# The decay sums' store moved from SyncE's DMA queue to GpSimd's

## The chip, the cores and the metric

One core of a Trainium2 chip runs the whole program once. Its engines are TensorE (PE, with its weight loads as PEld), VectorE (DVE), ScalarE (ACT), GpSimd (POOL) and SyncE (SP). SP, ACT and POOL also issue DMAs, each from its own instruction stream; all DMAs are carried by the same 16 DMA engines. The metric is the device time of one execution in microseconds, as the median of the runs.

## The reference

A causal attention with a decay bias on 8 batches of 8 heads (576 positions, head size 64) feeds a gated feed-forward layer on all 4608 tokens (model size 512, inner size 1536):

```python
s_pos = np.maximum(s, 0.0)
cum = np.cumsum(s_pos, axis=-1)
bias = -(cum[:, :, :, None] - cum[:, :, None, :])
scores = np.where(causal, -1000000000.0, scores + np.minimum(bias, 0.0))
attn = softmax(scores)
x = (attn @ v) as (tokens, 512)
out = (sigmoid(x @ w_gate) * (x @ w_val)) @ w_out
```

The change concerns `cum`: one row of 576 running sums for each of the 64 heads.

## The kernel before

The program is written as one long Python function; a scheduler then decides the order of the instructions on each engine from the data dependencies, the buffers and its own estimate of times, within the marks that the code sets (`high_priority`, `keep_in_program_order`, `issue_after`). A line that moves to another engine can therefore change the order on all engines. The order that results is quoted below where it counts.

*Start.* L108 loads `s` (64 rows of 576) with SP. L162, L164 and L166 on DVE clip it, sum it along the row and subtract the middle value; the result is `rel`. L167 stores `rel` into the DRAM tensor `cum_d`. Head 0 takes its row straight from `rel` (L451, POOL copies row 0 to all 128 partitions). Every later head i loads its row from `cum_d` into partition 0 of a tile `cr` (L447, SP) and L451 spreads it. `rel`, `s_sb`, `cum` and the first `vsq` tiles share the two buffers of the tag `rl`.

*Attention.* `n_load` (L596, SP) brings q and k of a pair of heads, `load_v` (L463, L464, SP) brings v. For batch 0 (8 heads) `n_prep`, `n_s`, `n_max`, `n_turn` and `n_av` work in float32: transposes on PE (L614, evacuated on ACT by L618 to L621), scores (L631), a fused add and minimum on DVE (L643), the exponential on ACT (L644), transposes (L653, L654) and the products with v (L662). Later batches use float16 pairs: scores L489 and L491, DVE L529, ACT L530, products L562 to L567. v's squares (L184 loads on POOL's queue, L186 on ACT) give a scale for each batch.

*Weights.* The weights come as 64-bit floats. `load_weight` loads a block: for the gate and value matrices 128 columns of each, 512 KB and 512 KB, into one staging buffer. Blocks 0 and 1 are loaded by SP (L284), block 0 into `ws`, block 1 into a part of `w2all` that is not yet in use; the later ones by ACT's queue (L286, and L279 for the first half of a w_out block, with the staging buffers `t2f`, `w2all` and `ws` in turn). `decode_weight` (L298 on ACT, L299 to L301 on DVE) makes 32-bit floats of them, `column_bound` (L310 on PE, L313 on DVE) finds a scale, and `split_weight` (L337 on ACT, L338 on DVE) writes a high and a low float16 part. There are 12 blocks of gate and value and 6 of w_out.

*Feed-forward.* `ffn_in` multiplies a group of 256 tokens with one block (L714), a unit of 24 products or more, into a PSUM tile `gv` that has two buffers; L719 on ACT takes the tanh, and L721 on DVE multiplies and so empties the tile. For the first two groups L721 writes into `t2f`. `ffn_out` (L745) multiplies with w_out. Group 0 and 1 start while heads 9 and up are still in attention and weights still come in.

*Order at the start on SP.* The calls at the end of the function (L884 on) issue `n_load(0)`, the two weight blocks and `load_v(0)`; the scheduler put L167 between the two loads of block 1. SP issues in order, and an issue that waits holds back all behind it. [...]

Of the kernel before, what the change touches and what calls it, by code (L numbers as in the profile page):

```python
# [25 lines left out]
def tile_attention_then_gated_ffn(  # L26
# [11 lines left out]
    nc = tc.nc  # L38
# [97 lines left out]
    cum_d = dp.tile([NH, S], F32, name="cum_d")  # L136
# [27 lines left out]
    nc.vector.tensor_tensor_scan(cum, sp_sb, zero, 0.0, ALU.add, ALU.add)  # L164
    rel = wp.tile([NH, S], F32, tag="rl", name="rel")
    nc.vector.tensor_scalar(rel, cum, cum[:, S // 2 : S // 2 + 1], -1.0, ALU.subtract, ALU.mult)  # L166
    nc.sync.dma_start(cum_d, rel)  # L167


    vch = H * S * D // P // S  # L170
# [958 lines left out]
```

## Time and profile before

| | us |
|---|---|
| median of 3 runs | 1143.78 |
| lowest and highest | 1140.69, 1146.3 |
| the profiled execution | 1143.07 |
| its span, first to last instruction | 1141.3 |
| PE busy | 1091.1 |
| DVE busy | 829.2 |
| ACT busy | 753.0 |
| POOL busy | 201.2 |
| mean granted TensorE clock | 0.99 |

The span is that of the profiled execution, and all times of the trace count from its start. A row of the timeline has the start in us, the duration in us, the engine (SPq, ACTq and POOLq are their DMA issues), the line, the operation, what it writes and reads, and in brackets how long the engine idled before it and what ended that wait. A DMA's issue is shorter than the DMA: the data land later. The chain of waits follows the work that ended last back from the last instruction, each step to what released it.

### The profile page before, as it was taken

The numbers are of one execution on the slowest core, as the hardware profiler recorded it, in microseconds if no ns is written. First come the engines' busy times: TensorE is split into PE (matmuls) and PEld (weight loads), VectorE is DVE, ScalarE is ACT, GpSimd is POOL, SyncE is SP. The second block draws the span as 40 slices with busy tenths as digits, with TensorE's granted clock in tenths as the row PEclk, the third lists the DMA queues.
The fourth block names the chain that finished last, engine by engine and source line by source line (L and its number), as shares of the span: only waits on it lengthen the run. The fifth ranks groups of instructions, "written<-read, shape, count | busy, mean of one in ns | idle before, by whom it ended". The sixth has DMA issues, their size and how long they took to land.

```text
span 1141.3 us, 30312 instructions
## 1 busy us (share of the span) xinstructions
PE 1091.1 (96%) x11796; PEld 854.8 (75%) x11796; DVE 829.2 (73%) x2357; ACT 753.0 (66%) x1474; POOL 201.2 (18%) x471
## 2 busy tenths in 40 slices
PE   6897878899999999999999999999999999999998
PEld 4776766757787787788777777778877887787775
DVE  6758989876787777766565577777777779682854
ACT  5868667767786777676656577768776666343533
POOL 3302101022232222221111112212121212000000
PEclk9999889999999999999999999999999999999999
DMA  9776896997989798775736469787977664200000
GB/s 270 215 206 140 180 165 144 183 186 163 174 176 173 158 177 162 155 152 116 169 66 149 103 152 164 150 166 156 179 134 164 145 117 93 41 20 2 20 1 37
DMA packets 445357, 157.62 MB, mean 138 GB/s; under 512 B 403551, under 2 KB 435295, under 8 KB 445214
## 3 DMA queue, kind: packets, MB, share of 16 engines
q1 hardware_dynamic: 418974, 128.17, 57.6%
q10 hardware_dynamic: 23040, 16.78, 5.0%
q0 software_dynamic: 3200, 10.75, 2.6%
q8 instruction: 92, 1.51, 0.5%
q14 instruction: 51, 0.42, 0.1%
HBM read 56.92 MB, written 9.58 MB: 58 GB/s over the span
## 4 chain that ended last, share of the span: by engine, by line
PE 70%; DMA 9%; DVE 8%; issue 5%; ACT 4%; SPq 2%; POOL 1%; ACTq 0%; POOLq 0%; DVEq 0%
PE gv L714 33%; PE o L745 21%; PE tv L831 3%; PE s L491 3%; PE s L489 2%; DMA v<-in_v_dram 2%; PE ta L831 1%; DVE e L529 1%; PE av L564 1%; PE av L562 1%; PE av L563 1%; PE na_ps L662 1%; DMA T<-qk 1%; DMA w2all<-in_moe_w_out_dram 1%; DMA x<-x 1%
## 5 line engine op out<-in xcount | busy, mean ns | idle before, releaser
L714 PE MATMUL gv<-x,w 128*128 128x256 f16 (+3 forms) x6336 | 553.9, 245 | 9.8 <-DVE t2f L721 8.8
L714 PEld LDWEIGHTS <-w 128*128 128x128 f16 x6336 | 480.2, 98 | 63.4 <-issue 12.0
L745 PE MATMUL o<-w2all,h 128*128 128x512 f16 x1296 | 313.9, 379 | 1.9 <-ACT h L729 1.9
L530 ACT ACTIVATE e<-e,em 128x576 f32<-128x576 f32 x280 | 153.1, 556 | 88.8 <-DVE em L529 86.0
L745 PEld LDWEIGHTS <-h 128*128 128x128 f16 x1296 | 123.4, 98 | 109.1 <-ACT h L729 2.3
L511 POOL TENSOR_SCALAR_AFFINE_SELECT rl<-rl 128x128 f32<-128x128 f32 (+1 forms) x240 | 88.4, 369 | 499.2 <-DVE em L529 456.2
L529 DVE CUSTOM_DVE_ANT_0 e<-s,rl,qkcf 128x576 f32<-128x576 f32 x280 | 151.2, 544 | 28.8 <-PE s L491 12.8
L729 ACT ACTIVATE h<-t,hsc 128x256 f16<-128x256 f32 x192 | 96.3, 503 | 92.7 <-DVE t L721 90.4
L719 ACT ACTIVATE th<-gv,scb 128x256 f32<-128x256 f32 (+3 forms) x264 | 99.0, 403 | 65.5 <-PE gv L714 53.9
L539 DVE SCALAR_TENSOR_TENSOR p<-e,p 128x384 f16<-128x384 f32 x224 | 103.2, 499 | 41.1 <-ACT p L534 40.3
L721 DVE SCALAR_TENSOR_TENSOR t<-th,gv 128x256 f32<-128x256 f32 x168 | 69.7, 415 | 63.9 <-ACT th L719 63.8
L534 ACT ACTIVATE p<-e 128x1152 f16<-128x1152 f32 x112 | 111.9, 1000 | 3.4 <-DMA pt<-p 0.9
L730 DVE SCALAR_TENSOR_TENSOR h<-t,hsc,h 128x256 f16<-128x256 f32 x192 | 93.4, 487 | 27.4 <-ACT h L729 25.0
L562 PE MATMUL av<-v,pt 128*128 128x65 f16 x560 | 67.7, 193 | 2.5 <-DMA pt<-p 2.5
L451 POOL PARTITION_BROADCAST cr<-cr x63 | 59.4, 949 | 55.9 <-ACT th L719 21.1
L489 PE MATMUL s<-T 128*128 128x288 f16 (+2 forms) x246 | 64.5, 280 | 3.8 <-DVE em L529 3.0
L563 PE MATMUL av<-v,pt 128*128 128x64 f16 x560 | 67.7, 192 | 0.0
L564 PE MATMUL av<-v,pt 128*128 128x65 f16 x560 | 67.6, 194 | 0.0
L491 PE MATMUL s<-T 128*128 128x288 f16 (+2 forms) x246 | 61.5, 277 | 4.0 <-DMA T<-T 4.0
L562 PEld LDWEIGHTS <-pt 128*128 128x128 f16 x560 | 52.5, 98 | 8.3 <-DMA pt<-p 3.4
L563 PEld LDWEIGHTS <-pt 128*128 128x128 f16 x560 | 52.5, 97 | 4.5
L564 PEld LDWEIGHTS <-pt 128*128 128x128 f16 x560 | 52.7, 97 | 0.2
(209 smaller groups left out, 1539.9 us busy)
## 6 DMA issues: line engine op xcount, KB each, us to landing
v<-v SPq DMA_DIRECT2D x56, 162.5 KB
v<-in_v_dram SPq DMA_DIRECT2D x64, 128.0 KB
out_dram<-io POOLq DMA_DIRECT2D x32, 256.0 KB, 3.4
T<-T SPq DMA_DIRECT2D x82, 72.0 KB
t2f<-in_v_dram SPq DMA_DIRECT2D x20, 288.0 KB
qk<-in_q_dram SPq DMA_DIRECT2D x17, 288.0 KB
qk<-in_k_dram SPq DMA_DIRECT2D x17, 288.0 KB
w2all<-in_moe_w_gate_dram ACTq DMA_DIRECT2D x7, 512.0 KB
```

What stands on the lines that cost most here:

```text
L491: nc.tensor.matmul(ps[:, : b_ - a], lhs, T[i][:, 2, a:b_], start=False, stop=not mask)
L529: nc.vector.tensor_tensor_reduce(e, ps, r, c, MASKED, ALU.add, ALU.min, acc)
L530: nc.scalar.activation(e_t[t][:, :w], e_t[t][:, :w], AF.Exp, bias=acc, scale=-1.0)
L534: nc.scalar.activation(p_s[h_][:, 0], e_s[h_], AF.Copy, scale=PSCALE)
L539: nc.vector.scalar_tensor_tensor(flat[:, LOW[t] * P : (LOW[t] + t) * P], e_t[t][:, : t * P], PSCALE, flat[:, kb * P : (kb + t) * P], ALU.m ...
L562: nc.tensor.matmul(AV[i][:, t], hi, v_[:, D : 2 * D + 1], start=kb == 0, stop=False)
L563: nc.tensor.matmul(AV[i][:, t, 0:D], hi, v_[:, 0:D], start=False, stop=False)
L564: nc.tensor.matmul(AV[i][:, t], lo, v_[:, D : 2 * D + 1], start=False, stop=False)
L714: nc.tensor.matmul(ps[:, gv, a:e], w1[f][:, cc, gv, wl], x_of(b, cc)[:, xl, c0 + a : c0 + e], start=(c == 0), stop=(c == 3 * NC - 1))
L719: nc.scalar.activation(th[:, a:e], ps[:, 0, a:e], AF.Tanh, scale=scb[b][:, f : f + 1])
L729: nc.scalar.activation(h[:, 0], t2, AF.Copy, scale=hsc[:, f : f + 1])
L745: mm = nc.tensor.matmul(ps[:m], h[:, hl, tt * P : tt * P + m], w2[f][:, wl], start=(f == 0 and c == 0), stop=(f == NF - 1 and c == 2))
```

## The change

L167 is issued by GpSimd instead of SyncE. Nothing else in the source changes; what is computed and the bytes moved are the same.

```diff
     rel = wp.tile([NH, S], F32, tag="rl", name="rel")
     nc.vector.tensor_scalar(rel, cum, cum[:, S // 2 : S // 2 + 1], -1.0, ALU.subtract, ALU.mult)
-    nc.sync.dma_start(cum_d, rel)
+    nc.gpsimd.dma_start(cum_d, rel)
```

The scheduler finds a new order for the whole front of the program. On SP, at the start (`nqk` is q or k of a pair of heads, `v_0` and `v_1` are v of the first two pairs, `cr` the rows of sums):

```order
 L284 DMA w2all<-in_moe_w_gate_dram 128x4x256
-L167 DMA cum_d<-rel 64x576
 L284 DMA w2all<-in_moe_w_val_dram 128x4x256
 L463 DMA v_0_159<-in_v_dram 128x4x64 x2
 L464 DMA v_0_159<-in_v_dram 64x2x64
+L463 DMA v_1_256<-in_v_dram 128x4x64
 L596 DMA nqk_251<-in_q_dram 96x6x64 x2
 L596 DMA nqk_251<-in_k_dram 96x6x64 x2
-L463 DMA v_1_256<-in_v_dram 128x4x64 x2
+L463 DMA v_1_256<-in_v_dram 128x4x64
 L464 DMA v_1_256<-in_v_dram 64x2x64
 L447 DMA cr_196<-cum_d 1x576
```

L167 is gone from between the two loads of block 1, and one of the loads of `v_1` stands ahead of the second pair's q and k. L167 now stands on POOL, directly ahead of head 0's L451 and of the first `vsq` load.

On ACT, where the fourth and fifth of w_out's blocks are loaded (into `w2all` and `t2f`), before:

```order
L534 ACTIVATE p_0_81<-e_79 128x768
L719 ACTIVATE th_8_1735<-gv_8_1710,scb_1272 128x256
L279 DMA t2f<-in_moe_w_out_dram 128x8x128
L286 DMA t2f<-in_moe_w_out_dram 128x8x128
L337 ACTIVATE w2all<-io,wscale 128x1024
L502 ACTIVATE rl_2784<-cr_2678,qkcf_2664 128x576
L502 ACTIVATE rl_2915<-cr_2795,qkcf_2664 128x576
L279 DMA w2all<-in_moe_w_out_dram 128x8x128
L286 DMA w2all<-in_moe_w_out_dram 128x8x128
```

and of the change:

```order
L534 ACTIVATE p_0_81<-e_79 128x768
L279 DMA w2all<-in_moe_w_out_dram 128x8x128
L286 DMA w2all<-in_moe_w_out_dram 128x8x128
L583 ACTIVATE x_4_2746<-xq_2260 128x640
L298 ACTIVATE io<-ws_146 128x1024
L279 DMA t2f<-in_moe_w_out_dram 128x8x128
L286 DMA t2f<-in_moe_w_out_dram 128x8x128
L719 ACTIVATE th_8_1735<-gv_8_1710,scb_1272 128x256
```

The `w2all` load has changed places with the `t2f` load.

On DVE, the rows from unit 10 to unit 11 of the first token group (L721 empties a unit's PSUM tile), before:

```order
L721 SCALAR_TENSOR_TENSOR t2f<-th_10_1793,gv_10_1768 128x256
L299 TENSOR_SCALAR w2all<-wa_147 128x1024
L300 SCALAR_TENSOR_TENSOR io<-io,w2all 128x1024
L300 SCALAR_TENSOR_TENSOR wa_147<-wa_147,w2all 128x1024
L721 SCALAR_TENSOR_TENSOR t2f<-th_11_1821,gv_11_1796 128x256
```

and of the change, from the second L300 on:

```order
L300 SCALAR_TENSOR_TENSOR wa_147<-wa_147,w2all 128x1024
L573 TENSOR_SCALAR er_2992<-av_2951 128x5
L529 ISA e_79,em_0_2923<-s_0_2901,rl_2784,qkcf_2664 128x64
L529 ISA em_0_2923 128x1
L338 SCALAR_TENSOR_TENSOR w2all<-io,wscale,w2all 128x1024
L301 SCALAR_TENSOR_TENSOR wa_147<-w2all,wa_147 128x1024
L574 RECIPROCAL er_2992<-er_2992 128x5
L313 TENSOR_SCALAR wj_1897,wtot_1896<-wps_1887 128x128
L539 SCALAR_TENSOR_TENSOR p_1_82<-e_80,p_1_82 128x384
L539 SCALAR_TENSOR_TENSOR p_1_82<-e_80,p_1_82 128x512
L547 SCALAR_TENSOR_TENSOR p_1_82<-e_80,p_1_82 128x2x64
L721 SCALAR_TENSOR_TENSOR t2f<-th_11_1821,gv_11_1796 128x256
```

Ahead of this piece, and behind unit 10's L721, the change also has L299 and the L529 of two other tiles. More rows of attention and of the weights stand between the two L721.

On PE the last difference between the two programs, and its end:

```order
 L714 MATMUL gv_5_5366<-x_143,w_5_71 128x256
-L714 LDWEIGHTS w_5_71
-L714 MATMUL gv_5_5366<-x_143,w_5_71 128x256
-L714 LDWEIGHTS w_5_71
-L714 MATMUL gv_5_5366<-x_2620,w_5_71 128x256
-L714 LDWEIGHTS w_5_71
-L714 MATMUL gv_5_5366<-x_2620,w_5_71 128x256
 L489 LDWEIGHTS T_5052
 L489 MATMUL s_4_5341<-T_5052 128x288
```

Three products of unit 5 of the fourth group (`gv_5_5366`) have moved behind the scores of a head; behind this place PE's order is the same in both.

## The prediction, made before the changed kernel was run

> **What bounds the kernel now.** I first read the head of the page for the span, then a table by stage, to see where TensorE is without work. The table cuts the span where the kind of work changes; its columns are the stretch in us, its length, busy time and instruction count of PE, PEld, DVE, ACT and POOL, the granted clock, the DMA share and GB/s.
>
> ```profile
> span 1141.3 us, 30312 instructions
> ```
>
> ```profile
> core 0: us, PE busy (x) PEld busy (x) DVE busy (x) ACT busy (x) POOL busy (x), PEclk, DMA share, GB/s
> 0.00:100.00 100.00, 81.37 (x580) 65.41 (x580) 68.89 (x191) 73.02 (x150) 26.25 (x60) 0.97 0.77 216
> 100.00:160.00 60.00, 48.64 (x527) 41.42 (x526) 58.40 (x166) 46.25 (x74) 5.08 (x8) 0.94 0.78 158
> 160.00:250.00 90.00, 78.15 (x787) 59.02 (x787) 76.60 (x224) 64.53 (x121) 11.76 (x24) 0.96 0.89 174
> 250.00:350.00 100.00, 97.47 (x1186) 74.48 (x1185) 74.37 (x224) 74.19 (x152) 25.98 (x56) 1.00 0.89 174
> 350.00:960.00 610.00, 608.13 (x7013) 479.90 (x7013) 438.67 (x1311) 418.07 (x821) 125.38 (x314) 1.00 0.72 146
> ```
>
> The reader is to see three things. From 350 to 960 us PE is busy 608.13 of 610: that stage only passes on what comes into it. TensorE's idle time lies before 250 us: 18.63 + 11.36 + 11.85 = 41.84 us of the 250. And from 100 to 160 us the full engine is DVE, 58.40 of 60. So whatever this change does is worth what it does to those 41.84 us. The order of instructions bears this out: the two programs differ on every engine at the front, but the last difference on PE lies in the sixth up-projection unit of the fourth token group, whose bank is emptied by the eighteenth L721 outside the first two groups, below; behind it both issue the same instructions in the same order. A gain or loss made before 350 us arrives at the end almost whole, and none can arise after it except by chance.
>
> ```profile
> 349.98 0.41 DVE L721 SCALAR_TENSOR_TENSOR t<-th,gv 128x256 f32<-128x256 f32 x1
> ```
>
> Now the place of the edit: the first 25 us.
>
> ```profile
> 4.74 0.51 SPq L284 DMA_DIRECT2D w2all<-in_moe_w_gate_dram  x1
> 7.67 0.48 SPq L167 DMA_DIRECT2D cum_d<-rel  x1
> 8.20 0.59 SPq L284 DMA_DIRECT2D w2all<-in_moe_w_val_dram  x1
> ...
> 11.60 3.41 SPq L596 DMA_DIRECT2D nqk<-in_q_dram  x1
> ```
>
> ```profile
> 0.74 3.10 DMA s_sb<-in_s_dram
> ...
> 8.20 7.67 DMA w2all<-in_moe_w_val_dram
> ```
>
> ```profile
> 15.89 1.12 ACT L298 ACTIVATE w2all<-w2all 128x1024 f32<-128x1024 f32 x1 [3.56 <-DMA w2all<-in_moe_w_val_dram]
> ```
>
> SP's queue stands still from 5.25 (4.74 + 0.51) to 7.67, because L167 waits for DVE to finish `rel`; the value half of the second weight block, next in the queue, is issued at 8.20. In the chain that ended last its transfer lasts 7.67 us, and ScalarE idles 3.56 us for it before decoding the block, with head 0's exponentials queued behind. So the wait that the edit removes lies on the path.
>
> **The change part by part.** *The wait on SP.* Without L167 the load is issued at about 5.25, 2.95 us sooner. [...] The best end is that it lands 2.95 us sooner, at 12.9. The other end comes from what SP's DMA queue had to do meanwhile. These are the bytes that it moved in 0 to 8 us and in 8 to 13 us (the columns are packets, MB, share of the engines), and what was issued on it in the first:
>
> ```profile
> q1 hardware_dynamic: 3204, 1.50, 71.8%
> ...
> ws<-in_moe_w_gate_dram SPq DMA_DIRECT2D x1, 512.0 KB
> ws<-in_moe_w_val_dram SPq DMA_DIRECT2D x1, 512.0 KB
> w2all<-in_moe_w_gate_dram SPq DMA_DIRECT2D x1, 512.0 KB
> nqk<-in_q_dram SPq DMA_DIRECT2D x2, 144.0 KB
> nqk<-in_k_dram SPq DMA_DIRECT2D x2, 144.0 KB
> s_sb<-in_s_dram SPq DMA_DIRECT2D x1, 144.0 KB
> ```
>
> ```profile
> q1 hardware_dynamic: 1632, 1.49, 89.9%
> ```
>
> Ahead of L167 stood 3 x 512 + 5 x 144 = 2256 KB, 2.31 MB; 1.50 MB of it had gone by 8 us. The other 0.81 MB is 2.7 us of work at 1.49 MB in 5 us. The queue never ran dry while SP waited, so the late issue cost the transfers little; what really leaves the front of the value load is the 144 KB of `cum_d`, 0.147 MB / 0.298 = 0.5 us. That the queue was full, not starved, is also seen at 11.60, where an issue that elsewhere takes 0.5 us took 3.41. I take -0.5 us, and keep 0 and -2.95 for the range. That the `cum_d` bytes must still be carried, now on another queue beside, is why 0 stays possible.
>
> [...]
>
> *The issue on GpSimd.* POOL now issues `cum_d` when `rel` is ready, ahead of head 0's broadcast and of v's loads.
>
> ```profile
> 7.74 0.86 POOL L451 PARTITION_BROADCAST cr<-rel  x1
> 8.43 0.73 POOL L184 DMA_DIRECT2D vsq<-in_v_dram  x1
> 12.78 0.55 POOL L184 DMA_DIRECT2D vsq<-in_v_dram  x1 [3.61 <-DMA cum_d<-rel]
> ```
>
> ```profile
> 10.50 0.76 DVE L643 CUSTOM_DVE_ANT_0 e<-s,cr 128x576 f32<-128x576 f32 x1 [2.85 <-PE s L518]
> ```
>
> ```profile
> 26.61 0.69 ACT L186 ACTIVATE vsq<-vsq 128x576 f32<-128x576 f32 x1
> ```
>
> An issue there costs 0.55 to 0.73 us. The broadcast would end at 9.3 instead of 8.6; its reader on DVE starts at 10.50 and waits for PE, so 1.2 us of cover remain, and without that cover the cost would be 0.7. The second `vsq` load waits until `cum_d` has left `rel`'s buffer (12.78 now). How long `cum_d` takes on POOL's queue no row shows; the nearest are the `vsq` loads there, 3.2 to 6.9 us to landing, so 11.6 to 15.3. At worst that load is 2.5 us later, and its reader runs at 26.61, behind other work: hidden. Both cost 0.
>
> *What the scheduler moves.* The order of all engines is found anew, and three further moves count. SP issues half of `v_1` earlier, and one issue fewer stands ahead of the first `cr` load; POOL waited 4.07 us for that one, but its reader on DVE waited only 0.7 us for POOL, so I cost it at 0 (-0.7 at best). Then, on ScalarE, the `w2all` half of w_out's loads now goes ahead of the `t2f` one. Before, it came second:
>
> ```profile
> 156.40 0.55 ACTq L279 DMA_DIRECT2D t2f<-in_moe_w_out_dram  x1
> ...
> 159.74 3.79 ACTq L286 DMA_DIRECT2D w2all<-in_moe_w_out_dram  x1
> ...
> 171.08 1.14 ACT L298 ACTIVATE wa<-w2all 128x1024 f32<-128x1024 f32 x1 [2.82 <-DMA w2all<-in_moe_w_out_dram]
> ```
>
> ```profile
> 168.54 0.41 DVE L721 SCALAR_TENSOR_TENSOR t2f<-th,gv 128x256 f32<-128x256 f32 x1
> 172.25 0.69 DVE L299 TENSOR_SCALAR w2all<-wa 128x1024 int32<-128x1024 int32 x1 [3.30 <-ACT wa L298]
> 172.86 1.22 DVE L300 SCALAR_TENSOR_TENSOR io<-io,w2all 128x1024 int32<-128x1024 int32 x1
> ...
> 175.13 0.41 DVE L721 SCALAR_TENSOR_TENSOR t2f<-th,gv 128x256 f32<-128x256 f32 x1
> ...
> 181.10 0.40 DVE L529 CUSTOM_DVE_ANT_0 e<-s,rl,qkcf 128x192 f32<-128x192 f32 x1
> ...
> 182.33 1.16 DVE L539 SCALAR_TENSOR_TENSOR p<-e,p 128x384 f16<-128x384 f32 x2
> 183.41 0.28 DVE L547 SCALAR_TENSOR_TENSOR p<-e,p 128x128 f16<-128x128 f32 x1
> 183.61 1.28 DVE L338 SCALAR_TENSOR_TENSOR w2all<-io,wscale,w2all 128x1024 f16<-128x1024 f32 x1
> ```
>
> With 1 MB fewer ahead of it that load can land in time, and DVE's 3.30 us wait goes: -3.3 at best, 0 at worst. Against it stands the third move: on DVE the rows that empty the up-projection's PSUM banks (L721) stand later. Between the last two of the first group stood L299 and two L300, 2.9 us (172.25 to 175.13). Now there stand L299 (0.69), one L300 (1.22), L338 (1.28), L301 (1.2, as L300 on the same shape), the three smaller L529 (0.4 each, as the middle one shown), two L539 (1.16) and an L547 (0.28): 7.0 us, less 0.08 for each of ten overlaps, as 172.25 + 0.69 against 172.86 shows: 6.2 us. The up-projection has two such banks, so where DVE is the full engine TensorE stands 6.2 - 2.9 = 3.3 us longer. Waits of this kind are there already:
>
> ```profile
>   PE gv L714: 8.8, 6
> ```
>
> That row is from the view of L721: who waited for it, us and times, in 100 to 230 us. Least is 0, if TensorE has attention products to do meanwhile. The two moves meet on the same stretch of DVE: the wait that goes is room for the rows put ahead. I take both whole, -3.3 + 3.3 = 0.
>
> *Sum:* -0.5 + 0 + 0 + 0 = -0.5 us. The profiled execution itself took 1143.07 us, 1141.3 of span and 1.8 around it; that is 0.7 below the median of the three runs, 1143.78. 1143.07 - 0.5 = **1142.6 us**.
>
> **The rivals.** *No difference* is the forecast: on either side of it, the terms must pull together to be seen, and a measurement of this kernel cannot tell less than about 0.5%, 5.7 us, from no change. *Faster:* the load lands as much sooner as it is issued (-2.95), head 1 gains its 0.7, and the w_out wait goes (-3.3) with TensorE never held by a bank: -6.95, 1136.1 us. For it speaks that the chain runs through all three; against it, the full queue at 8 us, and that 3.3 us of DVE rows come ahead of L721. *Slower:* the later L721 rows hold TensorE. The place is the end of each of the two first token groups (24 units, 125 to 229 us), the price 3.3 us a group, 6.6 in all, with nothing gained elsewhere: 1149.7 us. It decides from the point where DVE has no idle time between those rows, as in 100 to 160 us; if DVE idles ahead of L721 the price is 0. *The change does not do what it says:* the load leaves earlier but lands at 15.9 all the same, since the DMA engines are full; then the start is worth 0, 1143.1 us, within the forecast.
>
> **How the numbers follow.** The forecast and the empty change together have 0.60, faster 0.20, slower 0.20. The two sides get the same since each needs one stretch of DVE to go one way. The range must leave out no more than 0.2 and takes in both ends of the costs, 1136.1 and 1149.7, with a little more above, as the reordering may cost at places that I did not price: 1136 to 1151. Over 0.5% of the median is below 1138.1 or above 1149.5; the rivals reach these only with nearly all of their terms, so the chances are 0.20, 0.60 and 0.20.
>
> **What would show it.** In the changed kernel's profile SP should issue the second value load at about 5.3; ScalarE's L298 on it should start between 12.9 and 15.4, and its start says which account of the queue holds. The broadcast of `rel` should end near 9.3, with DVE's first L643 still waiting for PE. ScalarE's 2.82 us wait at the w_out load should be gone. PE's wait for L721 in 100 to 230 us should be near 8.8 + 3.3, and PE's idle time before 350 us near 44.4. I am wrong if that idle time moves by more than 6 us, or if PE idles between 350 and 960.

## The result, and the profile after

| | median us | lowest to highest | runs |
|---|---|---|---|
| before | 1144.23 | 1140.12 to 1147.29 | 20 |
| after | 1150.51 | 1144.74 to 1154.92 | 20 |

The ratio of after to before is 1.0051, with a 95% interval of 1.0038 to 1.0064: the change costs about 6 us. One of before's 20 runs took 5687.02 us, and one of those beside f1 and f2 took 1408.19 at a clock of 0.752; neither is in a ratio here, nor in the range above. The profiled execution of after took 1149.6 us.

The page's head, and the table by stage that the prediction began with, of the kernel after (same columns):

```profile
span 1147.5 us, 30330 instructions
```

```profile
0.00:100.00 100.00, 85.17 (x603) 69.55 (x603) 68.87 (x191) 73.40 (x152) 26.04 (x61) 0.95 0.77 217
100.00:160.00 60.00, 42.00 (x459) 35.48 (x458) 56.87 (x159) 45.81 (x73) 15.75 (x9) 0.87 0.73 150
160.00:250.00 90.00, 79.02 (x771) 60.77 (x770) 76.27 (x226) 62.33 (x114) 12.81 (x22) 0.94 0.89 181
250.00:350.00 100.00, 97.14 (x1174) 73.63 (x1172) 72.64 (x216) 71.52 (x146) 26.75 (x57) 1.00 0.81 161
350.00:960.00 610.00, 608.83 (x7052) 481.07 (x7050) 437.14 (x1303) 419.75 (x826) 124.67 (x314) 1.00 0.73 147
```

The reader is to see: in the first 100 us PE is busier than before (85.17 against 81.37), from 100 to 160 us it is far less busy (42.00 against 48.64), and the column PEclk is lower in all three stages ahead of 250 us. From 350 to 960 us PE is as full as before (608.83 against 608.13). The row by which both programs have become one, L721 of the fourth group's sixth unit, now starts at

```profile
357.09 0.41 DVE L721 SCALAR_TENSOR_TENSOR t<-th,gv 128x256 f32<-128x256 f32 x1
```

instead of 349.98: 7.1 us late, and the span is 6.2 us longer.

The timeline at the start, of the kernel after:

```profile
5.48 0.51 SPq L284 DMA_DIRECT2D w2all<-in_moe_w_val_dram  x1
...
7.69 0.86 POOL L451 PARTITION_BROADCAST cr<-rel  x1
...
10.43 0.76 DVE L643 CUSTOM_DVE_ANT_0 e<-s,cr 128x576 f32<-128x576 f32 x1 [4.34 <-PE s L518]
...
14.14 0.55 POOL L184 DMA_DIRECT2D vsq<-in_v_dram  x1 [5.17 <-issue]
...
14.46 1.15 ACT L298 ACTIVATE w2all<-w2all 128x1024 f32<-128x1024 f32 x1 [2.11 <-DMA w2all<-in_moe_w_val_dram]
```

SP issues the value load at 5.48 instead of 8.20, and ScalarE decodes it at 14.46 instead of 15.89. The earlier issue is the move's doing. The earlier decode is not shown to be: DVE had `rel` ready at 6.09 in this execution and at 7.64 in before's, and both times occur with the store on either engine. In e2, an experiment below with L167 on SP, `rel` was ready at 6.09 too:

```profile
6.12 0.48 SPq L167 DMA_DIRECT2D cum_d<-rel  x1
6.65 0.59 SPq L284 DMA_DIRECT2D w2all<-in_moe_w_val_dram  x1
...
14.31 1.14 ACT L298 ACTIVATE w2all<-w2all 128x1024 f32<-128x1024 f32 x1 [2.08 <-DMA w2all<-in_moe_w_val_dram]
```

With an early `rel` the decode starts at 14.31 with the store on SP and at 13.63 to 14.66 in the 14 profiles with it on GpSimd: no gain. With a late one it starts at 15.89 and 15.87 on SP (before, e6) and at 12.94, 13.10 and 13.80 on GpSimd (e3, e7, f2): 2.1 to 2.9 us sooner. The loss of time comes later. TensorE's waits from 100 to 250 us (us in total, times, the longest), before:

```profile
PE gv L714 <- DVE t2f L721: 8.8, 6, 3.3
PE nx_ps L686 <- DVE x L689: 3.7, 1, 3.7
PE s L491 <- DMA T<-T: 2.6, 2, 1.9
PE av L562 <- DMA pt<-p: 2.5, 3, 1.1
PE o L745 <- ACT h L729: 1.9, 1, 1.9
```

and after:

```profile
PE av L562 <- DMA pt<-p: 6.9, 3, 3.4
PE av L562 <- DVE xq L577: 6.4, 1, 6.4
PE nx_ps L686 <- DVE x L689: 3.8, 1, 3.8
PE gv L714 <- DVE t2f L721: 3.3, 2, 2.9
PE gv L714 <- ACT x L688: 2.3, 1, 2.3
```

The wait for L721, which the prediction expected to grow, fell from 8.8 to 3.3 us. In its place stand one of 6.4 us for L577, which empties the PSUM tile of a head's products, and a longer one for the transposed attention weights `pt`.

To have idle time and clock in one number I use **TensorE's missing work**: over slices of 1 us, the sum of 1 − busy share × granted clock, from windows like those above. In us, from one profiled execution each (the kernels other than before and after are those of the experiments below):

| | 0–44 | 44–100 | 100–165 | 165–210 | 210–250 | 250–350 | sum |
|---|---|---|---|---|---|---|---|
| before | 15.37 | 6.29 | 17.84 | 7.32 | 4.49 | 2.53 | 53.84 |
| after | 9.60 | 9.86 | 22.59 | 10.70 | 5.16 | 2.86 | 60.77 |
| e1 | 13.92 | 5.69 | 18.82 | 7.83 | 4.64 | 2.30 | 53.20 |
| h1 | 8.95 | 10.26 | 18.56 | 7.83 | 5.72 | 3.60 | 54.93 |
| i2 | 11.61 | 11.38 | 22.26 | 5.17 | 3.43 | 4.98 | 58.83 |
| j1 | 8.59 | 8.86 | 23.25 | 8.45 | 5.21 | 4.44 | 58.79 |

The sum is 6.9 us larger after than before, which fits the span's 6.2. Of before's 53.84, idle time is 44.38 and lost clock 9.46; after has 46.66 and 14.11. So only 2.28 us of the loss are idle time and 4.65 are lost clock. The change is 5.8 us ahead at 44 us (15.37 − 9.60), has lost 3.6 of that by 100 us, and loses 8.1 more from 100 to 210 us.

The same sums over the profiles of all the kernels below show what of this repeats. From 0 to 44 us the 14 kernels that follow after's order there have 8.4 to 11.6 us, and the five with before's 13.6 to 15.4. e2, with the store on SP, has 9.88, so the lead belongs to the order too. From 100 to 165 us after, e2, e3, e4, e6 and g1, all with after's order there but for single rows, have 22.6 to 23.3; before, e1, g4, h1 and h2, with before's order there, have 17.7 to 18.8. From 165 to 210 us the first six have 10.4 to 12.8, and the other five 7.3 to 8.9, but for g4 with 11.2; e7 and j1, after with rows moved in that stretch, have 7.5 and 8.5. From 44 to 100 us one execution says less, as g1 and h2 will show.

### The profile page after: what moved, and what is told of

Read it like the earlier page. It is cut to its first block, busy times and chain, and to the rows that moved or that the text cites. A ratio compares the mean times of both kernels' runs of the same rounds, so it can differ in the third digit from the quotient of the medians.

```text
span 1147.5 us, 30330 instructions
## 1 busy us (share of the span) xinstructions
PE 1094.8 (95%) x11796; PEld 858.7 (75%) x11796; DVE 830.2 (72%) x2357; ACT 753.9 (66%) x1474; POOL 214.3 (19%) x472
## 4 chain that ended last, share of the span: by engine, by line
PE 71%; DMA 8%; DVE 7%; issue 7%; ACT 5%; POOL 2%; SPq 1%; ACTq 0%; POOLq 0%; DVEq 0%
PE gv L714 32%; PE o L745 20%; PE tv L831 3%; PE s L491 2%; PE s L489 2%; DMA v<-in_v_dram 2%; DMA T<-qk 2%; PE na_ps L662 2%; PE ta L831 1%; DVE e L529 1%; PE av L564 1%; PE av L562 1%; PE s L631 1%; PE av L563 1%; POOL rl L511 1%
## 5 line engine op out<-in xcount | busy, mean ns | idle before, releaser
L529 DVE CUSTOM_DVE_ANT_0 e<-s,rl,qkcf 128x576 f32<-128x576 f32 x280 | 151.1, 545 | 35.4 <-PE s L491 16.5
L721 DVE SCALAR_TENSOR_TENSOR t<-th,gv 128x256 f32<-128x256 f32 x168 | 69.8, 416 | 61.1 <-ACT th L719 61.0
L451 POOL PARTITION_BROADCAST cr<-cr x63 | 71.3, 1138 | 62.8 <-DMA cr<-cum_d 49.0
```

The lines of the kernel that those rows point to most:

```text
L529: nc.vector.tensor_tensor_reduce(e, ps, r, c, MASKED, ALU.add, ALU.min, acc)
```

## The experiments

In the later kernels the order of each engine's instructions is held: behind the program a table lists, engine by engine, the instructions in the order wanted, and each is tied to the one ahead of it. Such a tie sets the order of issue. The ties by themselves cost nothing that the runs can tell: e1 below, tied to the order of before on every engine, has a ratio of 0.9994 (0.9975 to 1.0013). The code:

```python
for first_, then in zip(names, names[1:]):
    tc.add_manual_dep(traced[then], first_,
                      mybir.DependencyInfo(mybir.DependencyClass.NoSync, mybir.DependencyReason.DATA),
                      reason="order")
```

The ratios are to runs of the kernel before on the same chip beside them; the medians of these lie between 1143.88 and 1145.23 us.

### The line or the order (e1, e2)

Theory: the loss is the new order. Rival: the store itself, on GpSimd. e1 issues L167 on POOL and holds the order of before on every engine; e2 leaves L167 on SP, between the two loads, and holds the order of after.

```diff
     # e1, against before
-    nc.sync.dma_start(cum_d, rel)
+    nc.gpsimd.dma_start(cum_d, rel)
...
+    hold_order()   # table: before
     # e2, against before
+    hold_order()   # table: after
```

> L167 on GpSimd, every other instruction in the order of the kernel before on every engine. Theory 'order': the loss is made by the new order of rows on VectorE and ScalarE between 100 and 160 us, which leaves TensorE two holes (112 to 119 and 151 to 157 us, 11.6 us in the changed kernel). Then this run is within 0.3% of the kernel before (ratio 0.997 to 1.003), these holes are not there, and the value half of weight block 1 is still issued near 5.5 us. Rival 'queue': the store on GpSimd's queue itself costs the time, by its issue or its packets. Then the ratio is near the changed kernel's, 1.005.

> The reverse: L167 on SyncE between the two loads of block 1, every other instruction in the order of the changed kernel. Theory 'order': ratio 1.004 to 1.008, with the hole at 151 to 157 us as in the changed kernel; the first value load is late again and the start loses about 1.5 us. Rival 'queue': ratio 0.998 to 1.002.

e1 took 1144.68 us in 12 runs, ratio 0.9994 (0.9975 to 1.0013); e2 took 1152.27 in 8, ratio 1.0060 (1.0038 to 1.0082). The line alone costs nothing that these runs can tell, and the order alone costs all of it, with the store still on SP. One part of e2's expectation did not come: the value load was not late again, since `rel` was ready sooner (6.65 us, above). ScalarE's decode of the value block in e1's timeline:

```profile
13.88 1.15 ACT L298 ACTIVATE w2all<-w2all 128x1024 f32<-128x1024 f32 x1 [2.08 <-DMA w2all<-in_moe_w_val_dram]
```

That is 2.0 us sooner than in before's profile, with `rel` ready at 6.09 here as well, and worth nothing that these runs can tell.

### The two longest new stalls, one at a time (e3, e4)

Theory: the wait of 6.4 us for L577, or those for L689 and L688, are the loss. Rival: the next row in the queue takes their place. Rows of the held order, e3 on DVE and e4 on ACT and DVE, against the order of after:

```diff
 L573 TENSOR_SCALAR er_2742<-av_2701 128x5
+L574 RECIPROCAL er_2742<-er_2742 128x5
+L577 TENSOR_TENSOR xq_2260<-av_2701,er_2742 128x5x64
 L338 SCALAR_TENSOR_TENSOR w_10_76<-w2all,wscale,w_10_76 128x8x128
...
 L338 SCALAR_TENSOR_TENSOR w_11_77<-w2all,wscale,w_11_77 128x8x128
-L577 TENSOR_TENSOR xq_2260<-av_2701,er_2742 128x5x64
```

```diff
 L534 ACTIVATE p_0_81<-e_79 128x768
+L688 ACTIVATE x_142<-nx_ps_0_1225,vsc_339 128x320
...
 L415 SCALAR_TENSOR_TENSOR qkcf_1268<-qksc_1266 128x1
+L689 SCALAR_TENSOR_TENSOR x_142<-nx_ps_0_1225,vsc_339,x_142 128x320
```

> The changed kernel with two rows of VectorE moved: L574 and L577 of head 9, which free the one PSUM tile av, stand directly behind L573. Theory 'order': TensorE's 6.4 us wait for that L577 near 151 us goes or falls below 3 us, no half clock follows it, and the time falls by 3 to 8 us below the changed kernel's 1150.5, to 1142 to 1147 (ratio to the kernel before 0.998 to 1.003). Rival 'full engine': VectorE is the bound from 105 to 160 us, so the hole only moves to the next row that TensorE needs: 1149 to 1152, ratio 1.004 to 1.007.

> The changed kernel with two rows moved: the first half of head pair 3's output, L688 on ScalarE up by six rows to behind L534, and L689 on VectorE up by 17 rows to behind L415; both empty the same PSUM tile. Theory 'order': TensorE's waits of 2.3 and 3.8 us for them near 112 to 119 us go, the half clock of 113 to 124 us goes, and the time falls by 2 to 6 us to 1144.5 to 1148.5 (ratio 1.000 to 1.004). Rival 'full engine': TensorE runs on to its next wait for VectorE, the first L721, which cannot move, and the time stays at 1149 to 1152.

e3: 1152.06 us in 10 runs, 1.0061 (1.0039 to 1.0083). e4: 1151.62 in 10, 1.0056 (1.0036 to 1.0077). Neither gained. TensorE's waits from 100 to 165 us, of e3 and of e4:

```profile
PE gv L714 <- DVE t2f L721: 7.2, 2, 7.0
```

```profile
PE av L562 <- DVE xq L577: 6.7, 1, 6.7
PE wps L310 <- DVE w L299: 5.8, 2, 4.6
PE s L489 <- DMA T<-qk: 4.1, 1, 4.1
```

In e3 the wait for L577 is gone, and L721 holds TensorE at the same place for 7.0 us; in e4 the waits for L689 and L688 are gone, and L299 and a `T` stand in their place. A name in the list of waits is only the row that came last; the rows behind it were nearly as late.

### Which stretch of the order (e5, e6, g4, h1)

Theory: the rows behind 100 us cost. Rival: those at the start do. The table follows one order up to a time t of its own profile, and then takes what is left in the other order.

```diff
-    hold_order()   # table: after
+    hold_order()   # g4: after to 20 us, then before; e5: to 44; h1: to 100
+    hold_order()   # e6, L167 on SP: before to 100 us, then after
```

> L167 on GpSimd; the changed kernel's order only up to what had begun at 20 us, the order of the kernel before behind that. The cut at 44 us gave 1.0051, with a wait of 3.4 us of TensorE for ScalarE's L619 at the seam. If the new rows of 20 to 44 us and that seam did the harm, this is 0.996 to 1.001; if any departure from the old order costs (rival), 1.003 to 1.006.

> L167 on GpSimd; every engine follows the changed kernel's order up to what it had begun at 44 us, and the order of the kernel before from there. Theory 'order' with a lead: the changed start is 5.8 us ahead at 44 us (TensorE idle plus lost clock 9.6 against 15.4 us), and the loss comes later, so this run is faster than the kernel before by what of the lead survives 100 to 160 us: 0 to 5 us, ratio 0.995 to 1.000. Rival 'start': the new start itself does the harm (more prefetch and weight work early leaves later stages worse): ratio 1.003 or more.

> L167 on GpSimd; the changed kernel's order up to what had begun at 100 us, the order of the kernel before behind that (the mirror of the run with the old order to 100 us, 1.0086). At 100 us both kernels have done the same rows of VectorE but one and the same of ScalarE but three, so there is hardly a seam. Theory 'rows behind 100 us': TensorE's idle time plus lost clock of 100 to 160 us is 14 to 17 us as in the kernel before (22 in the changed kernel), ratio 0.997 to 1.002. Rival 'any departure from the old order': 1.004 to 1.008.

> L167 on SyncE; the order of the kernel before up to what had begun at 100 us, the changed kernel's order behind it. Theory 'order': the harm is in the rows behind 100 us (holes near 111 to 119 and 151 to 157 us), so the ratio is 1.004 to 1.010, and the sum of TensorE's idle time and lost clock before 350 us is 60 us or more against 53.8. Rival 'start': ratio 0.998 to 1.002.

| | order to t / behind | median us, runs | ratio |
|---|---|---|---|
| e1 | before / before | 1144.68, 12 | 0.9994 (0.9975 to 1.0013) |
| g4 | after to 20 / before | 1144.53, 12 | 1.0009 (0.9994 to 1.0024) |
| e5 | after to 44 / before | 1149.52, 12 | 1.0051 (1.0032 to 1.0070) |
| h1 | after to 100 / before | 1145.97, 12 | 1.0004 (0.9989 to 1.0019) |
| e6 | before to 100 / after | 1153.93, 6 | 1.0086 (1.0066 to 1.0107) |
| after | after / after | 1150.51, 20 | 1.0051 (1.0038 to 1.0064) |

The rows behind 100 us carry the loss: with after's start and before's rest (h1) no loss can be told, and with the reverse (e6) more is lost than in after. e5 looks like a witness for the start, but at its seam, near 47 us, TensorE waits 3.4 us for ScalarE's L619, which neither order has by itself; h1 contains the same start without that seam.

### Emptying the PSUM tiles first (e7, e8, g3)

Theory: DVE rows that hold a PSUM tile (L689, L721, L574, L577) stand behind rows of the weights that nobody waits for, and moving all of them up from 100 to 250 us repairs the order. e7 moves 37 such rows in after's order, e8 36 in e5's, g3 36 in e1's.

```diff
-    hold_order()   # table: after (e7), e5 (e8), before (g3)
+    hold_order()   # the same, each such DVE row up to where the trace has its input ready
```

> The changed kernel with 37 of VectorE's rows between 100 and 250 us (L689, L721, L574, L577, which empty PSUM tiles) moved up to the first place behind the row that was running when their input was ready; nothing else moves. In the last runs a single such row moved up only let TensorE run on to the next one. Theory 'weight rows first': the holes exist since L299 to L301 and L338, 0.7 to 1.3 us each, stand ahead of these rows, and moving all of them gives back the loss: 1138 to 1146 us, ratio 0.995 to 1.002. Rival 'full engine': VectorE has as much to do as before and the holes only move, 1148 to 1153, ratio 1.003 to 1.008.

> The first kernel of this series (new order to 44 us, old order behind) with 36 such rows moved up in the same way. Theory 'weight rows first': 3 to 8 us below that kernel, 1132 to 1140 us, ratio 0.990 to 0.997. Rival 'full engine': the same as that kernel within 2 us.

> L167 on GpSimd, the order of the kernel before, with 36 of VectorE's rows from 100 to 250 us that empty PSUM tiles moved up as in the kernel with the new start (there the move took the mean from 1149.5 to 1145.5). Theory 'weight rows first': 2 to 5 us below the kernel before, ratio 0.995 to 0.998, faster than both. Rival 'full engine' or 'the old order is a local best': 0.999 to 1.003.

e7: 1148.96 us in 8 runs, 1.0044 (1.0024 to 1.0063). e8: 1144.33 in 12, 1.0014 (0.9995 to 1.0034). g3: 1143.91 in 12, 0.9998 (0.9983 to 1.0013). In after's order the move brought 1.5 us by the mean, which the intervals can't tell from nothing; in before's order nothing. Against e5, e8 is 4 us better by the mean (1145.5 against 1149.5); part of that may be e5's seam, so it isn't evidence for the rule.

### Filling TensorE's holes behind 100 us (f1, f2)

Theory: the half clock (a granted clock of 0.50) behind the holes is the loss, so products without use in the holes keep the clock up and bring the time back. Rival: DVE sets the pace there, and more work on PE costs. f1 adds 60 products of 128x512 to after in five holes, f2 adds 37 to e1; they write into the tile of a later column bound, which overwrites them.

```diff
+    def warm(ps, n):
+        x = w1[0].rearrange("p c g l n -> p (c g l n)")
+        for _ in range(WARM.get(n, 0)):
+            nc.tensor.matmul(ps, x[:, :P], x[:, :512], start=True, stop=True)
```

> The changed kernel, same order on every engine, with 60 extra matmuls (128x512 float16, into a PSUM tile that the next column bound overwrites, waiting for nothing) in TensorE's queue just ahead of five instructions at which it stands still: 8 and 12 ahead of the waits of 112 to 119 us, 22 ahead of the one at 151 to 157, 9 at 174 to 177, 9 at 196 to 198; at the 0.22 us that such a product takes they fill 60 to 75% of each hole. No wait gets shorter by them. Theory 'clock': what the changed order costs is not the holes but the half clock that follows them. Time less lost clock, (1 - clock) x span, was 1131.7 to 1134.4 us on average in all ten kernels so far, and lost clock 11.2 us in the kernel before, 18.6 in the changed one. Then filled holes keep the clock: mean clock 0.988 or more, 1141 to 1147 us, ratio 0.997 to 1.002. Rival 'holes': the idle time itself is the cost, and the extra work can only add: 1150 to 1156, ratio 1.005 to 1.010, clock 0.984 as before.

> L167 on GpSimd with the order of the kernel before (the first run of this series, ratio 0.9994), and 37 such matmuls ahead of the five waits of that order: 12 at 111 to 115 us, 6 at 123 to 125, 5 at 149 to 151, 9 at 158 to 161, 5 at 171. Theory 'clock': of the 12 us of lost clock 5 to 8 go: 1136 to 1141 us, ratio 0.993 to 0.998, faster than both. Rival 'holes': 1144 to 1149.

f1: 1156.71 us in 6 runs, 1.0098 (1.0074 to 1.0121). f2: 1151.29 in 7, 1.0055 (1.0032 to 1.0078). The mean clock over the runs rose, from 0.9838 (after) to 0.9888 and from 0.9895 (e1) to 0.9913, and both kernels are slower than without, by 6.0 and 6.9 us of the mean; f2 came out slower than either theory or rival had it. So a higher clock behind those holes is no gain in itself. In f1's profile the stage 250 to 350 us, full in both kernels above, has room in it:

```profile
250.00:350.00 100.00, 94.37 (x1131) 72.03 (x1130) 68.13 (x204) 67.25 (x140) 24.87 (x53) 0.97 0.72 150
```

Why the added products leave TensorE short of work there was not settled.

### The start: where the lead goes (g1, h2)

Theory: the lead of 5.8 us at 44 us is lost to the clock. The windows on both sides of 51 us, before and after:

```profile
44.00:51.00 7.00, 7.00 (x54) 5.83 (x54) 5.19 (x17) 6.96 (x17) 1.79 (x4) 1.00 1.10 345
51.00:63.00 12.00, 10.22 (x81) 8.41 (x80) 8.13 (x22) 9.58 (x21) 3.01 (x5) 1.00 0.54 154
```

```profile
44.00:51.00 7.00, 5.42 (x43) 4.11 (x42) 3.48 (x12) 6.28 (x14) 3.18 (x5) 1.00 0.78 243
51.00:63.00 12.00, 10.39 (x50) 8.93 (x48) 5.66 (x11) 6.73 (x14) 0.49 (x2) 0.57 0.52 145
```

After has small holes at 47 to 49 and 51 to 53 us (1.1 and 1.6 us idle). From 51.8 us on, inside the second, it has half clock, and over the window a granted clock of 0.57: PE is as busy as before, with 50 products in place of 81. DVE and ACT are half idle there, so this stretch is TensorE's. g1 puts ten products into these holes in after, h2 into h1.

```diff
+            warm(bank[0], i, t)   # ten products, ahead of head 4's first scores, which overwrite them
```

> The changed kernel with 10 extra matmuls (128x512 float16, into the score tile of head 4 before its first use) in TensorE's queue: 2, 2 and 6 ahead of the waits of 0.7, 0.6 and 1.6 us between 47 and 53 us. In the changed kernel's trace these small holes are followed by 10.4 us of half clock (51 to 63 us) in which TensorE is busy throughout, 5.1 us lost; the lead of the start, 5.8 us at 44 us, is gone by 100. Theory 'lead lost': the clock stays at 1.0 from 51 to 63 us and the time falls by 2 to 5 us below the changed kernel's 1150.3 mean, to 1145 to 1148, ratio 1.001 to 1.004. Rival 'later stage decides': VectorE, full from 105 to 160 us, takes the lead back whatever comes before it: 1149 to 1152, ratio 1.004 to 1.007, though the clock at 51 to 63 is 1.0.

> The same with the 10 extra matmuls between 47 and 53 us, which kept the clock there and left TensorE 6 us further at 100 us. Theory 'rows behind 100 us' with a lead that survives: 2 to 5 us below the run before this one, 1138 to 1142, ratio 0.994 to 0.998, faster than both kernels. Rival 'the full VectorE takes the lead': within 2 us of the run before this one.

The same window, of g1 and of h2:

```profile
51.00:63.00 12.00, 11.36 (x85) 9.54 (x85) 9.95 (x25) 8.81 (x19) 0.94 (x4) 1.00 0.62 163
```

```profile
51.00:63.00 12.00, 11.30 (x84) 9.29 (x83) 10.24 (x26) 9.12 (x20) 0.76 (x3) 1.00 0.61 163
```

The clock is 1.00 in both and the products are back. One profile alone doesn't show that the added products did it, since this half clock does not come in every execution. Of the ten profiled kernels with after's order to 100 us and nothing added before that, eight lose 3.4 to 6.8 us of clock between 49 and 66 us, and two, e3 and i1, lose none. The window of i1:

```profile
51.00:63.00 12.00, 10.01 (x77) 8.29 (x77) 9.71 (x26) 9.86 (x20) 1.03 (x4) 1.00 0.65 176
```

What shows it is the mean clock over 12 runs each: 0.9895 in h1 and 0.9936 in h2, or 12.0 and 7.3 us of lost clock. g1: 1149.04 us in 8 runs, 1.0037 (1.0016 to 1.0057), 1.7 us better than after by the mean, which the intervals can't tell from nothing. h2: 1141.84 in 12, 0.9977 (0.9963 to 0.9992), 3.5 us better than h1 by the mean, and **faster than both kernels**, if only by 0.2%. The new start was a gain; in most executions (eight of those ten profiles) the half clock at two small holes had taken it.

### Where behind 100 us (i1, i2, j1)

Theory: the two largest new holes, 112 to 119 and 151 to 157 us, are the loss. Rival: they are given back, and the loss lies behind them. i1 and i2 are h1 with the cut at 130 and at 165 us. j1 is after with one row of SP moved: head 11's `pt` transpose ahead of four others.

```diff
-    hold_order()   # h1: after to 100 us, then before
+    hold_order()   # i1: to 130; i2: to 165
     # j1, rows of SP against after
 L436 DMA T<-qk
+L550 DMA pt<-p
 L441 DMA T<-T
 L442 DMA T<-T
 L585 DMA x<-x
 L436 DMA T<-qk
-L550 DMA pt<-p
```

> L167 on GpSimd; the changed kernel's order up to what had begun at 130 us, the order of the kernel before behind that. It contains the changed order's stretch with TensorE's waits of 112 to 119 us and not the one of 151 to 157. Cut at 100 us the ratio was 1.0004, uncut 1.0051. If both stretches share the loss: 1.001 to 1.004; if the second alone makes it: 0.999 to 1.001; if the first alone: 1.004 to 1.006.

> The same with the cut at 165 us, behind the wait of 151 to 157. If the loss is made between 100 and 165 us: 1.004 to 1.007, as uncut; if the rows behind 165 us have a share: 1.001 to 1.004.

> The changed kernel with one row moved, on SyncE's queue: head 11's transposed probabilities (L550, pt, issued at 170.41 us) stand ahead of L441, L442, L585 and L436 instead of behind them. Their input was ready at 162.7 us. In the changed kernel TensorE waits for them from 173.7 to 177.1 us, and VectorE, which is the full engine there, waits 4.58 us for scores queued behind; cut at 165 us the changed order cost 1.0013, uncut 1.0051. Theory 'unpaid stall': only a wait in which VectorE itself stands still is lost for good, and this is the one that the cut removed. Then its 4.58 us falls below 2, and the time falls by 3 to 5 us, to a mean of 1145.3 to 1147.3, ratio 1.001 to 1.003. Rival 'many small losses behind 165 us': within 1.5 us of the changed kernel, ratio 1.004 to 1.006.

i1: 1147.41 us in 12 runs, 1.0013 (0.9992 to 1.0034). i2: 1147.49 in 12, 1.0013 (0.9990 to 1.0036). Both holes are in i2 as in after; its waits of TensorE from 100 to 210 us begin

```profile
PE av L562 <- DVE xq L577: 6.6, 1, 6.6
PE s L491 <- DMA T<-T: 4.6, 3, 1.8
PE nx_ps L686 <- DVE x L689: 3.8, 1, 3.8
PE gv L714 <- ACT x L688: 2.3, 1, 2.3
```

and yet i2 can't be told from before. The windows, of before, after and i2:

```profile
100.00:165.00 65.00, 52.49 (x546) 44.08 (x545) 61.41 (x175) 48.41 (x77) 5.08 (x8) 0.91 0.82 162
165.00:210.00 45.00, 38.77 (x440) 32.90 (x439) 41.38 (x109) 31.05 (x51) 5.02 (x8) 0.98 0.82 166
```

```profile
100.00:165.00 65.00, 46.98 (x498) 39.51 (x497) 61.87 (x173) 47.51 (x76) 19.92 (x10) 0.87 0.76 161
165.00:210.00 45.00, 37.65 (x412) 31.52 (x413) 39.27 (x110) 29.28 (x48) 2.84 (x6) 0.92 0.83 168
```

```profile
100.00:165.00 65.00, 47.17 (x509) 40.26 (x509) 60.63 (x171) 48.62 (x78) 8.18 (x10) 0.87 0.72 150
165.00:210.00 45.00, 39.83 (x435) 34.38 (x434) 40.78 (x109) 29.13 (x50) 4.13 (x5) 1.00 0.85 169
```

From 100 to 165 us DVE is busy 60.6 to 61.9 of 65 in all three, so TensorE's larger holes in after and i2 come with about the same amount of DVE work, in another order. In i2 the next stage gives some of it back (missing work 5.17 there, against 7.32 before and 10.70 after), though its sum to 350 us, 58.83, stays 5 us above before's. In after, DVE too falls to 39.27 of 45 there. The largest new stall of that stage is SP's doing. In after:

```profile
164.93 0.47 SPq L441 DMA_DIRECT2D T<-T  x1
165.45 0.59 SPq L442 DMA_DIRECT2D T<-T  x1
166.13 1.82 SPq L585 DMA_TRANSPOSE x<-x  x1
168.05 2.31 SPq L436 DMA_TRANSPOSE T<-qk  x1
170.41 1.31 SPq L550 DMA_TRANSPOSE pt<-p  x1
```

```profile
177.09 0.20 PE L562 MATMUL av<-v,pt 128*128 128x65 f16 x1 [3.40 <-DMA pt<-p]
...
178.19 0.55 DVE L529 CUSTOM_DVE_ANT_0 e<-s,rl,qkcf 128x320 f32<-128x320 f32 x1 [4.58 <-PE s L518]
```

TensorE waits 3.40 us for `pt`, whose transpose stood behind four other issues, and DVE then 4.58 us for TensorE's scores. In j1:

```profile
160.72 1.46 SPq L550 DMA_TRANSPOSE pt<-p  x1
```

```profile
174.89 0.55 DVE L529 CUSTOM_DVE_ANT_0 e<-s,rl,qkcf 128x320 f32<-128x320 f32 x1 [1.08 <-PE s L518]
```

The transpose is issued 9.7 us sooner, DVE's wait falls to 1.08, and the time stays: 1149.92 us in 11 runs, 1.0050 (1.0025 to 1.0074). (The profile is of j1's fastest run, 1146.47 us; the mean is 1150.9, so its row in the table above is better than typical.) So that stall isn't the loss either.

**What is shown and what is open.** Shown: the loss is the order, it needs after's rows behind 100 us, and repairing any one of the named stalls brings nothing that these runs can tell, that is, not more than 2 or 3 us. With the cut at 165 us the ratio is 1.0013, uncut 1.0051; the two intervals just part (1.0036 and 1.0038), and a cut also makes a seam, so that most of the loss lies behind 165 us is likely rather than shown. Which rows there it is, or whether it is many small ones, stays open.

## Why the prediction failed, by its own steps

- *What bounds the kernel, and that a gain or loss before 350 us arrives at the end:* right. The lag is 7.1 us at L721 and 6.2 at the end, and PE is busy 608.83 of 610 behind 350.
- *The wait on SP, −0.5 with bounds of 0 and −2.95:* the issue came at 5.48 as expected, right behind the one ahead of it (4.75 + 0.68 us), and L298 at 14.46, in the stated window of 12.9 to 15.4. But the stretch in which SP stood still was read from one execution. With `rel` late, as there, L298 starts 2.1 to 2.9 us sooner, near the bound; with `rel` early, as in e2 and after, no sooner. At the end of the kernel e1 allows −2.9 to +1.5 us, so −0.5 can be told neither from 0 nor from the bounds.
- *The issue on GpSimd, 0:* right. The broadcast ended at 8.55, sooner than the 9.3 expected, L643 still waited for PE, and the second `vsq` load went out at 14.14 with its reader far behind.
- *The w_out load, −3.3:* the wait of 2.82 us on ScalarE went as said, ScalarE's L298 and DVE's L299 starting without it:

```profile
171.65 1.15 ACT L298 ACTIVATE wa<-w2all 128x1024 f32<-128x1024 f32 x1 [0.22 <-issue]
172.93 0.68 DVE L299 TENSOR_SCALAR w2all<-wa 128x1024 int32<-128x1024 int32 x1
```

  but DVE then waits 4.58 us at 178.19, and in j1, where that wait falls to 1.08, the time stays.
- *L721 later, +3.3:* wrong. The rows ahead of the last L721 of the first group came as priced, about 6.7 us of them between 172.60 and 184.29 (6.2 were named), but TensorE did not wait for it there: it waited for `pt`. Its wait for L721 was to be near 12.1 us and was 3.3.
- *The step that failed* is "What the scheduler moves": three moves were priced, and all others entered the sum as 0 by being left out. In its place the runs showed that the new order as a whole costs 0.6%, about 7 us, with the store still on SP (e2), by rows that the sum doesn't hold: in the profiles TensorE's missing work from 100 to 210 us grows by 8.1 us, while the wait for L721, the one loss that was priced, fell. Which rows make it stays open. It was luck that the time fell inside 1136 to 1151: only a little added above, for "places that I did not price", let it in.
- *The rival "slower"* came, with 1149.7 named and 1150.51 measured, but not by its mechanism: L721's wait fell. Another PSUM tile, L577's, held TensorE for 6.4 us, and e3 shows that this alone isn't the price.
- *The chain*, which for the rival "faster" was to run through all three of its gains, passes in before's profile through the value load and the w_out load. From 23 to 25 us it runs over ScalarE's L654, L286, L618 and L619, not over head 1's broadcast.
- *The sign that was to show an error*, idle time moving by over 6 us, was the wrong one: idle time moved by 2.28 and lost clock by 4.65. The prediction shows the column PEclk and prices it in no term.

## What to carry to other kernels

Under a scheduler a one-line move is a new order for every engine: hold the old order with the new line and the new order with the old line before looking for a cause in either, and cut the order by time before repairing rows. A hole in one engine where another is full may be a loan that is given back, so the row that a view of waits names there is not yet a cost: e3, e4 and j1 each removed the named wait and gained nothing that could be told. Where TensorE is the engine that sets the pace, look at the granted clock behind small holes: ten products without use in two of them were worth 3.5 us in h2, while 60, 42 of them where DVE was full, cost 6 us in f1. And read a wait or a half clock in several executions before pricing it: `rel` came 1.5 us earlier or later at the start, and the half clock at 51 us came or stayed away, in kernels with the same order there.

## What the runs showed of the hardware

In windows of 1 us the granted clock fell to 0.50 in stretches whose lost clock, the sum of 1 − granted clock, was 1.70 or 1.71 us or two or three times that. In the profile after these are 51 to 63 us (5.12 lost), 113 to 124 (5.12), 154 to 162 (3.42), and 178 to 182, 198 to 203 and 239 to 243 (1.71 each); in before 16 to 21, 34 to 38, 115 to 120 and 126 to 130 us (1.70 or 1.71 each) and 160 to 168 (3.42). At a clock of 0.50, 1.71 us lost are about 3.4 us of half clock, by my estimate from these sums.

The idle time ahead of a fall differed. In after the clock fell at 239.5 us behind one hole that began 1.9 us earlier, and at 51.8 us with only 1.2 us of idle time in the 3.4 us before it (48.4 to 51.8 us). In before, holes of 1.84, 1.93 and 1.89 us (at 149, 199 and 218 us) passed without a fall. What makes the clock fall behind one hole and not behind another as long was not shown.

In these runs the time of a kernel went with its mean clock. Taking (1 − clock) × span off the mean time leaves 1133.6 us for before (over the 150 runs beside the experiments, clock 0.9902, 11.1 lost), 1131.7 for after (0.9838, 18.6 lost) and 1134.6 for h2 (0.9936, 7.3 lost); all kernels but f1 and f2 lie between 1130 and 1135. That is a correlation and no cause: every stretch of half clock named above has idle time ahead of it, and f1 and f2 had a higher clock and took longer.
